# The hand-over between two layers: the first chunk's return trip from memory in two other tiles, and the second chunk's scalings at another place of the last unit

## The chip, the cores and the metric

The kernel runs on one core of one Trainium2 chip. A core has five engines that run side by side, each through its own list of instructions in order: TensorE (PE, with its weight loads shown as PEld), VectorE (DVE), ScalarE (ACT), GpSimd (POOL) and SyncE (SP), which here issues nearly all transfers. The metric is the device time of one execution in microseconds (us); the kernel before has a median of 1962.9 us over 3 runs (1961.62 to 1962.97).

## What is computed

Two layers, each an attention with one shared key and value head and a SwiGLU feed-forward, with a layer norm ahead of each and a residual sum behind it. There are 2048 positions of 448 features, 16 query heads of 28, and a hidden width of 1792.

```python
def _A_ref(x, wq, wk, wv, wo):
    q = (x @ wq).reshape(B, S, H, Dh).transpose(0, 2, 1, 3)
    k = x @ wk
    v = x @ wv
    scores = jnp.einsum("bhqd,bkd->bhqk", q, k) * (Dh ** -0.5)
    p = _softmax(scores, axis=-1)
    o = jnp.einsum("bhqk,bkd->bhqd", p, v)
    return o.transpose(0, 2, 1, 3).reshape(B, S, H * Dh) @ wo

def _B_ref(x, w_gate, w_up, w_down):
    return (_silu(x @ w_gate) * (x @ w_up)) @ w_down

x = A_x
x = x + _A_ref(_layernorm(x), A_wq, A_wk, A_wv, A_wo)
x = x + _B_ref(_layernorm(x), B_w_gate, B_w_up, B_w_down)
x = x + _A_ref(_layernorm(x), A_wq, A_wk, A_wv, A_wo)
x = x + _B_ref(_layernorm(x), B_w_gate, B_w_up, B_w_down)
```

## The kernel before

**Tiling.** The 2048 positions are four chunks `c` of 512, each four tiles of 128 positions. The residual stream stays on chip in `xres`. A product with a weight needs the chunk normalised and turned, features on the partitions, as a high and a low part (`xh`, `xl`) whose sum is the value. A chunk is turned in one of two ways. `flip` turns it on TensorE: the four tiles are scaled into a tile `xn` (line 255 on DVE, with a copy of the last 64 features on POOL, line 257), then for each of four feature slices k four transposes go into one PSUM bank (line 296), and `flipped` takes the high part from the bank on ACT (line 304) and the low part on DVE (lines 309, 312). The other way goes through memory: DVE transposes 32x32 blocks into `xn` (line 260), four transfers write them out to `xt` (line 269), `load` brings them back (line 273), and `cut` makes high and low parts of what came back.

**The feed-forward.** 1792 hidden columns are 14 blocks `fc` in 7 groups of two. In groups 2 to 5 the work is arranged in another way (`blocked`), which uses the four `keys` tiles as operands. Group 6, the last, runs as single units: for each chunk c, for n = 0 and 1, `unit` makes the gate and up products of one block (line 350), then the SiLU on ACT (line 1110), the product with the up half on DVE (line 1111, here called the gating), the high part of the result on ACT (line 1112) and its low part on DVE (line 1115). The down product of a unit is held back in `pend` and issued during the next unit.

**The hand-over.** When the last group of a layer has added a chunk to `xres` and there is a next layer, `hand_over` prepares that chunk for the next attention. Chunk 0 goes through memory: its block transposes come one unit later and its `load` two units later, through a list `soon` whose entries count down at the end of each unit; its `cut` stands in `mid` of the very last unit (group 6, chunk 3, n = 1). Chunk 1 is flipped on TensorE: its four scalings are the function `ready`, and it too has a place in `soon`. The last unit's entry in `soon` that comes first is the one with the first three projections of the next layer.

`unit` runs the list of the place `mid` between the two halves of its gate and up products:

```python
for f in mid[:1]:
    f()
first.pop(0)()
for f in mid[1:]:
    f()
```

and the list `soon` at its end, in the order in which entries were added:

```python
for e in list(self.soon):
    e[0] -= 1
    if e[0] < 0:
        self.soon.remove(e)
        e[1]()
```

**The next layer's projections.** `project` takes pairs (chunk, m) in the order m = 3, 2, 0, 1 of each chunk. Each is 11 matmuls into one bank (line 330). ACT copies the bank to a `stage` tile (line 558), SP sends it to memory as `qd` (line 559) and, for m = 3 and 2, its last rows as `kt` (line 562); for m = 0 and 1 DVE transposes the last rows into `vt` (line 565) and POOL files them in `vsb` (line 568). There are two `stage` tiles, so a third copy waits until the transfers from the first have landed. Ahead of the fourth projection, `turned` flips chunk 1. After that comes the held-back down product of the last unit, and then the projections of chunks 1 to 3.

**What sets the order.** The order on each engine is the order in which the program issues the instructions; nothing reorders them. The banks of a unit and of the projections are taken in turn from a list of four.

**Tiles.** `xn` is a single buffer: each new use of it waits until every reader of the last use is done. `keys` are four tiles of [128, 2, 512], allocated for the whole program. In the next layer the split of `keys[2]` and `keys[3]` comes with its projections 15 and later.

Of the kernel before, what the change touches and what calls it, by code (L numbers as in the profile page):

```python
# [8 lines left out]
F32 = mybir.dt.float32  # L9
# [6 lines left out]
P = 128  # L16
# [36 lines left out]
def forward(  # L53
# [14 lines left out]
    nc = tc.nc  # L68
# [9 lines left out]
    pers = ctx.enter_context(tc.tile_pool(name="pers", bufs=1))  # L78
# [47 lines left out]
    def rows3(dst, src):  # L126
        nc.sync.dma_start(dst[:, 0:3], src[0:384, :].rearrange("(k p) n -> p k n", p=P))
        for rs in (slice(0, 64), slice(64, 128)):
            nc.sync.dma_start(dst[rs, 3], src[384:448, :])
# [18 lines left out]
    keys = [pers.tile([P, 2, 512], F32R, name=f"keys{c}") for c in range(NC)]  # L148
# [77 lines left out]
    def xtile(pool, again=None):  # L226

        return (
            pool.tile([P, 4, 512], F32R, name="xh"),
            pool.tile([P, 3, 512], F32R, name="xl"),  # L230
            again,
        )

    def norm_steps(c, away=None, n=1):


        got = {}

        def stat(t):
            nc.vector.bn_stats(stats[:, 4 * c + t, :], xres[:, 4 * c + t, :])  # L240
            nc.vector.bn_aggr(mv[:, 4 * c + t, :], stats[:, 4 * c + t, :])

        def scale(z):
            m = 4 // n
            rstd = pers.tile([P, 4], F32, name="rstd", bufs=2)[:, 0:m]
            nc.gpsimd.tensor_scalar(rstd, mv[:, 4 * c + m * z : 4 * c + m * z + m, 1], 1.0, EPS, ALU.mult, ALU.add)
            nc.gpsimd.tensor_tensor(rstd, rstd, halfn[:, 0:m], ALU.pow)
            got["r"] = got.get("r", []) + [rstd[:, t : t + 1] for t in range(m)]

        def apply(t):  # L250
            if t == 0:
                got["x"] = pers.tile([P, 4, 512], F32, name="xn")
            got["o"] = (away() if away else got["x"][:, t, :])[:, 0:D]
            i, r = xres[:, 4 * c + t, :], got["r"][t]
            nc.vector.tensor_scalar(got["o"], i, mv[:, 4 * c + t, 0:1], r, ALU.subtract, ALU.mult)
            if not away:
                nc.gpsimd.tensor_copy(got["x"][:, t, D:512], got["o"][:, 384:D])

        def turn(t):
            nc.vector.transpose(side()[:, :, :, t], got["o"].rearrange("p (k s) -> p k s", s=32))  # L260

        def side():
            return got["x"].rearrange("p t n -> p (t n)")[:, 0 : 4 * D].rearrange("p (k s t) -> p k s t", s=32, t=4)

        def send():
            turns.append(dram.tile([D, 512], F32, name=f"xt{len(turns)}"))
            got["xt"] = turns[-1]
            for a in range(4):
                nc.sync.dma_start(
                    got["xt"].rearrange("(k r) n -> r k n", r=32)[:, :, P * a : P * a + P],  # L270
                    side()[32 * a : 32 * a + 32].rearrange("p k s t -> p k (s t)"),
                )

        def load():
            got["raw"] = pers.tile([P, 4, 512], F32, name="xn")
            rows3(got["raw"], got["xt"])

        got["load"] = load
        fs = [lambda t=t: stat(t) for t in range(4)] + [lambda z=z: scale(z) for z in range(n)]
        for t in range(4):  # L280
            fs += [lambda t=t: apply(t)] + [lambda t=t: turn(t)] * bool(away)
        return fs + [send] * bool(away), got
# [3 lines left out]
    def cut(got, tiles, ks=range(4), copy=nc.scalar.copy):  # L286

        for k in ks:
            flipped(tiles, k, got["raw"][:, k, :], copy)

    def flip(got, tiles, ks=range(4)):

# [6 lines left out]
    def flipped(tiles, k, pt, copy, steps=(0, 1)):  # L299

        xh, xl, xd = tiles
        twice = xd if k == 3 else None
        if 0 in steps and twice is None:
            copy(xh[:, k, :], pt)
        elif 0 in steps:
            copy(xh[0:64, k, :], pt[0:64, :])
            copy(xd[64:128, :], pt[64:128, :])
        if 1 in steps and k < 3:
            nc.vector.tensor_tensor(xl[:, k, :], pt, xh[:, k, :], ALU.subtract)
        elif 1 in steps:  # L310
            high = xh[64:128, k, :] if twice is None else xd[64:128, :]
            nc.vector.tensor_tensor(xh[64:128, k, :], pt[64:128, :], high, ALU.subtract)
# [470 lines left out]
    class FeedForward:  # L783
# [251 lines left out]
        def hand_over(self, gi, c):  # L1035

            a = self.nxt
            fs, got = norm_steps(c, None if c else lambda: qraw)
            for f in fs[:5]:
                f()  # L1040
            a.pool = self.stage
            a.X[c] = xtile(xpool if c < 2 else self.xbp)

            def ready():
                for f in fs[5:]:
                    f()
                a.norms[c] = got

            wipe = lambda: nc.gpsimd.memset(qraw, 0.0)
            if c == 0:  # L1050
                self.soon.append([1, lambda: [f() for f in fs[5:9]]])
                self.soon.append([2, lambda: [f() for f in (*fs[9:], got["load"], wipe)]])
                self.mid[gi, 3, 1] = [lambda: None, lambda: cut(got, a.X[c])]
                self.soon.append([5, lambda: [a.project() for _ in range(3)]])
            elif c == 1:
                self.soon.append([3, ready])
            else:
                a.plan[4 * c - 4, 0] = [ready]

# [121 lines left out]
        def rest(self, xb):  # L1181
# [10 lines left out]
            if mixed:  # L1192
                self.lend(mixing)
            cut(self.norms[2], self.X[2])
            third, self.norms[3] = norm_steps(3)
            for f in third[:5]:
# [45 lines left out]
    fs, got = norm_steps(0, n=2)  # L1242
# [28 lines left out]
    for c in range(1, NC):  # L1271
        fs, got = norm_steps(c, n=2)
        n = 4 * c - 4 - (c == 3)
# [40 lines left out]
```

## Time and profile before

| | before |
|---|---|
| median of 3 runs | 1962.9 us (1961.62 to 1962.97) |
| the profiled execution | 1962.7 us |
| its span, first to last instruction | 1960.9 us |
| granted TensorE clock, mean | 1.000 |
| ACT busy | 1339.3 us (68%) |
| DVE busy | 1016.9 us (52%) |
| POOL busy | 771.3 us (39%) |
| transfers | 79.69 MB, mean 41 GB/s |

Times inside the execution are us from the span's start. A row of the timeline reads: start, duration, engine, line of the program, operation, what is written and what is read, shapes, number of instructions merged into the row, and in brackets how long the engine sat idle before it and what released it. A row with several instructions spans from the first one's start to the last one's end. "SPq" rows are issues of transfers; how long the data then take is not in the row. The hand-over from the first layer to the second lies between 960 and 1006 us.

### The profile page before, as it was taken

The page shows a single profiled execution, that of the slowest core. Times are in us where ns is not written, and L with a number is a line of the kernel's source. Part 1 is how long each engine was busy: PE and PEld are TensorE (multiplying, and loading weights), DVE is VectorE, ACT ScalarE, POOL GpSimd, SP SyncE. Part 2 cuts the span into 40 slices and gives each one's busy share as a digit, 9 for nine tenths or more (in the row PEclk, how much of TensorE's full clock was granted, in tenths as well). Part 3 has the DMA queues.
Part 4 walks back from the last instruction along what each step waited for, and adds up shares of the span by engine and source line. Part 5 has one row for each costly group of instructions (what it writes and reads, how often), then busy time and mean ns, then how long its engine had stood idle before and what let it go on. Part 6 is the DMA issues. An engine that isn't in the chain of part 4 may idle for free. (4 is left out here: it accounts for less than half of the span.)

```text
span 1960.9 us, 45644 instructions
## 1 busy us (share of the span) xinstructions
PE 1947.1 (99%) x18307; PEld 1319.9 (67%) x18307; DVE 1016.9 (52%) x1711; ACT 1339.3 (68%) x2353; POOL 771.3 (39%) x997
## 2 busy tenths in 40 slices
PE   9999999999999999999999999999999999999998
PEld 8544545445458999999974444454444688999997
DVE  7434543544435567665654335435444346667653
ACT  4899797998964344444349998979979533444432
POOL 5212111132314868766341221111222167688640
PEclk9999999999999999999999999999999999999999
DMA  5111020121210110011131111102112101110102
GB/s 168 53 30 26 25 49 20 32 59 28 73 33 2 53 33 24 24 33 27 52 112 33 29 31 31 45 12 61 31 50 50 33 6 49 33 32 22 27 17 77
DMA packets 100001, 79.69 MB, mean 41 GB/s; under 512 B 26024, under 2 KB 82984, under 8 KB 99784
## 3 DMA queue, kind: packets, MB, share of 16 engines
q1 hardware_dynamic: 99208, 75.81, 14.3%
q8 instruction: 144, 2.36, 0.5%
q10 hardware_dynamic: 576, 0.92, 0.1%
q14 instruction: 73, 0.60, 0.1%
HBM read 57.15 MB, written 18.74 MB: 39 GB/s over the span
## 5 line engine op out<-in xcount | busy, mean ns | idle before, releaser
L672 PE MATMUL bank<-pt,vsb 128*32 128x512 f32 x4096 | 493.3, 598 | 0.3
L631 PE MATMUL bank<-qstack,keys 32*128 32x512 f32 x1536 | 484.7, 425 | 0.0
L631 PE MATMUL three<-qstack,keys 32*128 32x512 f32 x4608 | 460.6, 425 | 1.5 <-DVE vt L565 1.2
L631 PEld LDWEIGHTS three<-qstack,keys 32*128 32x128 f32 x4608 | 254.4, 182 | 295.0 <-ACT pt L644 179.4
L638 ACT ACTIVATE pt<-three 128x1536 f32<-128x1536 f32 x256 | 372.1, 1454 | 1.2 <-PE bank L672 0.8
L644 ACT ACTIVATE pt<-three 128x1536 f32<-128x1536 f32 x256 | 371.7, 1452 | 0.0
L350 PE MATMUL bank<-xh,wgh 64*128 64x512 f32 x1344 | 364.5, 392 | 0.3 <-DVE sg L1111 0.3
L350 PE MATMUL bank<-wdh,h 64*128 64x448 f32 x1776 | 329.4, 364 | 0.1
L640 DVE COPY raw<-bank 128x512 f32<-128x512 f32 x256 | 177.2, 692 | 226.9 <-PE bank L631 224.6
L350 PE MATMUL bank<-xh,wgl 64*128 64x512 f32 x1020 | 291.8, 390 | 0.0
L682 DVE TENSOR_TENSOR o<-bank,o 128x512 f32<-128x512 f32 x224 | 154.9, 691 | 239.5 <-PE bank L672 234.6
L672 PEld LDWEIGHTS bank<-pt,vsb 128*32 128x32 f32 x4096 | 107.1, 109 | 249.7 <-issue 153.0
L711 POOL TENSOR_TENSOR o<-o 128x512 f32<-128x512 f32 x32 | 41.2, 1287 | 592.6 <-DMA o<-rd 459.3
L357 ACT COPY seen<-bank 128x1 f32<-128x1 f32 x788 | 100.2, 163 | 243.4 <-PE bank L350 182.4
L350 PE MATMUL bank<-xl,wgh 64*128 64x512 f32 x912 | 254.9, 390 | 0.0
L631 PEld LDWEIGHTS bank<-qstack,keys 32*128 32x128 f32 x1536 | 243.4, 183 | 1.2 <-DVE o L682 0.6
L350 PEld LDWEIGHTS bank<-wdh,h 64*128 64x128 f32 x1776 | 237.7, 184 | 9.5 <-issue 2.0
L350 PE MATMUL bank<-wdl,h 64*128 64x448 f32 x888 | 213.2, 366 | 0.0
L350 PEld LDWEIGHTS bank<-xh,wgh 64*128 64x128 f32 x1344 | 200.3, 184 | 11.6 <-DVE sg L1111 0.7
L897 POOL TENSOR_TENSOR xres<-stage,xres 128x448 f32<-128x448 f32 x120 | 151.0, 1269 | 113.0 <-ACT stage L890 112.8
L643 ACT ACTIVATE pt<-bank 128x512 f32<-128x512 f32 x256 | 151.0, 590 | 61.1 <-PE bank L631 60.9
L862 DVE TENSOR_TENSOR xn<-bank,xn 128x512 f32<-128x512 f32 x192 | 126.5, 687 | 125.7 <-PE bank L350 94.7
(202 smaller groups left out, 3085.3 us busy)
## 6 DMA issues: line engine op xcount, KB each, us to landing
o<-rd SPq DMA_DIRECT2D x32, 256.0 KB
qraw<-qd SPq DMA_DIRECT2D x128, 56.0 KB
qd<-stage SPq DMA_DIRECT2D x30, 224.0 KB
xt<-xn SPq DMA_DIRECT2D x28, 224.0 KB
wdr<-in_B_w_down_dram SPq DMA_DIRECT2D x28, 224.0 KB
wr<-in_B_w_gate_dram SPq DMA_DIRECT2D x32, 192.0 KB
wr<-in_B_w_up_dram SPq DMA_DIRECT2D x32, 192.0 KB
xn<-xt SPq DMA_DIRECT2D x7, 768.0 KB
```

The costliest lines, as they stand in the source:

```text
L350: nc.tensor.matmul(po, a, b, start=start, stop=stop, skip_group_check=True)
L357: nc.scalar.copy(seen[:, i : i + 1], po[:, 0:1])
L631: nc.tensor.matmul(three[:, j, :] if j < 3 else one, k[js, kp, ks], q[js, part, :], start=(z == 0), stop=(z == 2), tile_position=(32 * j, 0),)
L638: nc.scalar.activation(pt, three, AF.Exp, scale=SCALE)
L640: nc.vector.tensor_copy(raw, one)
L643: nc.scalar.activation(pt1, one, AF.Exp, scale=SCALE)
L644: nc.scalar.activation(pt, three, AF.Exp, scale=SCALE)
L672: nc.tensor.matmul(po[32 * j : 32 * j + 32, :], vsb[:, n % NT, :], pts[n][j], start=(n == 2 * d), stop=(n > 2 * d), skip_group_check=True,)
L682: nc.vector.tensor_tensor(acc, in_turn(po), acc, ALU.add)
L711: nc.gpsimd.tensor_tensor(rb, oraw, rb, ALU.mult)
L862: plus = lambda out, po, r: tt(by_tile(out), in_turn(po), by_tile(r), ALU.add)
L897: nc.gpsimd.tensor_tensor(r, h[e, t], r, ALU.add)
```

## The change

`load` gets an argument. Without it, it does what it did. With two tiles it issues four transfers in the place of three: feature slices 0 and 1 of `xt` go to the first tile in one transfer, slice 2 to the second tile in one, and the 64 rows of slice 3 twice, to both halves of the partitions, as before. `hand_over` calls it for chunk 0 with `keys[2]` and `keys[3]`, and `cut` reads the slices from there. `ready`, the scalings of chunk 1, leaves `soon` and is appended to the list in `mid` of the last unit, behind the `cut` of chunk 0.

```diff
-        def load():
-            got["raw"] = pers.tile([P, 4, 512], F32, name="xn")
-            rows3(got["raw"], got["xt"])
+        def load(into=None):
+            if into is None:
+                got["raw"] = pers.tile([P, 4, 512], F32, name="xn")
+                rows3(got["raw"], got["xt"])
+                return
+            two, one = (t.bitcast(F32) for t in into)
+            nc.sync.dma_start(two, got["xt"][0:256, :].rearrange("(k p) n -> p k n", p=P))
+            nc.sync.dma_start(one[:, 0], got["xt"][256:384, :])
+            for rs in (slice(0, 64), slice(64, 128)):
+                nc.sync.dma_start(one[rs, 1], got["xt"][384:448, :])
+            got["apart"] = [two[:, 0], two[:, 1], one[:, 0], one[:, 1]]
...
-            flipped(tiles, k, got["raw"][:, k, :], copy)
+            flipped(tiles, k, got["apart"][k] if "apart" in got else got["raw"][:, k, :], copy)
...
-                self.soon.append([2, lambda: [f() for f in (*fs[9:], got["load"], wipe)]])
+                self.soon.append([2, lambda: [f() for f in (*fs[9:], lambda: got["load"](keys[2:4]), wipe)]])
                 self.mid[gi, 3, 1] = [lambda: None, lambda: cut(got, a.X[c])]
                 self.soon.append([5, lambda: [a.project() for _ in range(3)]])
             elif c == 1:
-                self.soon.append([3, ready])
+                self.mid[gi, 3, 1].append(ready)
             else:
                 a.plan[4 * c - 4, 0] = [ready]
```

On DVE, in the last unit of the first layer, the order was as follows. `bank_7095` holds the unit's up product, `bank_7094` the third projection, `h` is the unit's result, `vt` belongs to the third projection, and the rows behind it are chunk 1's.

```order
L309 TENSOR_TENSOR xl<-xn,xh 128x512 x3
L312 TENSOR_TENSOR xh<-xn,xh 64x512
L1111 TENSOR_TENSOR sg<-bank_7095,sg 128x512
L1115 TENSOR_TENSOR h_12398<-sg,h_12398 128x512
L565 STREAM_TRANSPOSE vt<-bank_7094 32x512
L255 TENSOR_SCALAR xn<-xres,mv,rstd 128x448 x4
L309 TENSOR_TENSOR xl<-bank_7095,xh 128x512
L309 TENSOR_TENSOR xl<-bank_7096,xh 128x512
```

With the change, in the same place:

```order
L317 TENSOR_TENSOR xl<-keys_97,xh 128x512 x2
L317 TENSOR_TENSOR xl<-keys_98,xh 128x512
L320 TENSOR_TENSOR xh<-keys_98,xh 64x512
L255 TENSOR_SCALAR xn<-xres,mv,rstd 128x448 x4
L1119 TENSOR_TENSOR sg<-bank_7095,sg 128x512
L1123 TENSOR_TENSOR h_12407<-sg,h_12407 128x512
L573 STREAM_TRANSPOSE vt<-bank_7094 32x512
L317 TENSOR_TENSOR xl<-bank_7095,xh 128x512
L317 TENSOR_TENSOR xl<-bank_7096,xh 128x512
```

The four scalings moved up past the third projection's `vt`, the unit's low part and its gating, to right behind the low parts of chunk 0. Lines below 273 read 8 higher in the changed program, and line 309 became 317.

SP's queue at the return trip, before:

```order
L269 DMA xt_12143<-xn 32x14x128 x4
L127 DMA xn<-xt_12143 128x3x512
L129 DMA xn<-xt_12143 64x512 x2
L559 DMA qd_0_12427<-stage 112x512
L562 DMA kt_0_800<-stage 12x512
L559 DMA qd_0_12427<-stage 112x512
```

and with the change:

```order
L269 DMA xt_12143<-xn 32x14x128 x4
L280 DMA keys_97<-xt_12143 128x2x512
L281 DMA keys_98<-xt_12143 128x512
L283 DMA keys_98<-xt_12143 64x512 x2
L567 DMA qd_0_12436<-stage 112x512
L570 DMA kt_0_800<-stage 12x512
L567 DMA qd_0_12436<-stage 112x512
```

One transfer of three slices became one of two and one of one; nothing behind them moved. TensorE's order is unchanged.

## The prediction

> **What bounds the kernel now.** I read the page's busy shares first, then TensorE's waits over the whole span.
>
> ```profile
> span 1960.9 us, 45644 instructions
> PE 1947.1 (99%) x18307; PEld 1319.9 (67%) x18307; DVE 1016.9 (52%) x1711; ACT 1339.3 (68%) x2353; POOL 771.3 (39%) x997
> ...
> PE bank L296 <- DVE xn L255: 2.1, 1, 2.1
> PE bank L1263 <- POOL ident masks.py:199: 1.9, 1, 1.9
> ```
>
> TensorE is busy for all but 1960.9 - 1947.1 = 13.8 us, and the change leaves its list of instructions alone. So only a gap can be won or made. The longest single wait on record, 2.1 us, is for the very scalings that move: line 296 flips chunk 1, line 255 scales it. The timeline of TensorE shows the place.
>
> ```profile
> 979.21 0.39 PE L330 MATMUL bank<-xh,wh 128*128 128x512 f32 x1
> 984.42 0.39 PE L330 MATMUL bank<-xh,wl 128*128 128x512 f32 x1
> 986.90 2.91 PE L296 MATMUL bank<-ident,xn 128*128 128x128 f32 x16 [2.09 <-DVE xn L255]
> 989.90 0.19 PEld L330 LDWEIGHTS bank<-xh,wh 128*128 128x128 f32 x1 [0.33 <-DVE xl L309]
> 989.90 0.50 PE L330 MATMUL bank<-xh,wh 128*128 128x512 f32 x1
> ```
>
> The third projection ends at 984.42 + 0.39 = 984.81. The 16 transposes begin 2.09 us later and are spread over 2.91 us, and the fourth projection starts at 989.90, held last by a low part (line 309). It takes chunk 0's operands, but its bank is the one that held chunk 1's first slice, so DVE must have read that slice first. From 984.81 to 989.90 are 5.09 us in which TensorE has 16 transposes to do. DVE shows why.
>
> ```profile
> 975.36 1.90 DVE L309 TENSOR_TENSOR xl<-xn,xh 128x512 fp32r<-128x512 f32 x3 [0.58 <-ACT xh L304]
> 977.29 0.69 DVE L312 TENSOR_TENSOR xh<-xn,xh 64x512 fp32r<-64x512 f32 x1
> 978.00 0.69 DVE L1111 TENSOR_TENSOR sg<-bank,sg 128x512 f32<-128x512 f32 x1
> 979.38 0.69 DVE L1115 TENSOR_TENSOR h<-sg,h 128x512 fp32r<-128x512 f32 x1 [0.69 <-ACT h L1112]
> 985.51 0.72 DVE L565 STREAM_TRANSPOSE vt<-bank 32x512 f32<-32x512 f32 x1 [5.44 <-ACT stage L558]
> 986.27 1.85 DVE L255 TENSOR_SCALAR xn<-xres,mv,rstd 128x448 f32<-128x448 f32 x4
> 989.15 1.89 DVE L309 TENSOR_TENSOR xl<-bank,xh 128x512 fp32r<-128x512 f32 x3 [1.04 <-ACT xh L304]
> ```
>
> DVE idles 5.44 us ahead of `vt`, which waits for the third projection, and the scalings are queued behind `vt`: they could have run in that idle time.
>
> **The change part by part.** First the scalings. They move to 977.29 + 0.69 = 977.98, behind the low part of chunk 0. What they read is there by then: the last statistic of chunk 1 leaves POOL at 975.14 + 1.03 = 976.17, and the writers of `xt`, which must have read the old `xn`, have landed before the load is issued at 969.58. The new tiles matter here: in the old `xn` the scalings would have had to wait for the readers of chunk 0 as well.
>
> ```profile
> 975.14 1.03 POOL L247 TENSOR_TENSOR rstd<-rstd,halfn 128x4 f32<-128x4 f32 x1
> 986.37 1.42 POOL L568 COPY vsb<-vt 32x64 f32<-32x64 f32 x4 [10.20 <-DVE vt L565]
> 987.85 0.89 POOL L257 COPY xn<-xn 128x64 f32<-128x64 f32 x4
> 969.58 0.38 SPq L127 DMA_DIRECT2D xn<-xt  x1
> 970.01 1.14 SPq L129 DMA_DIRECT2D xn<-xt  x2
> 980.53 0.32 SPq L559 DMA_DIRECT2D qd<-stage  x1
> 980.90 0.39 SPq L562 DMA_DIRECT2D kt<-stage  x1
> 983.38 0.42 SPq L562 DMA_DIRECT2D kt<-stage  x1
> 985.92 0.71 SPq L419 DMA_DIRECT2D few<-kt  x1
> ```
>
> They end at 977.98 + 1.85 = 979.83, POOL's four copies, now ahead of `vsb` on an engine idle for 10.20 us, about 0.9 us later: 4 us before TensorE asks.
>
> What sets the fourth projection's start then is a chain of rows that all stand here: third projection's end 984.81; its copy on ACT at 984.89; `vt` 0.62 later, 985.51; its end and hand-off 986.27. In the place of the scalings DVE then takes the low part of slice 0. In the trace that step reaches TensorE in 989.90 - 989.15 = 0.75. The start is 986.27 + 0.75 = 987.02 in the place of 989.90: **a gain of 2.88 us**, just the stretch from 986.27 to 989.15 that falls out. Two things must be done by 986.27 and 987.02. ACT's high part of slice 0 comes 0.63 after the first transpose where the flips are fed freely, and takes 989.15 - 988.54 = 0.61 to reach DVE.
>
> ```profile
> 1004.48 1.91 PE L296 MATMUL bank<-ident,xn 128*128 128x128 f32 x16
> 1005.11 2.05 ACT L304 CAST xh<-bank 128x512 fp32r<-128x512 f32 x4 [0.25 <-PE bank L296]
> 1006.14 0.47 PE L330 MATMUL bank<-xh,wh 128*128 128x512 f32 x1
> ```
>
> That is chunk 2, later on. With a first transpose at about 984.87 ACT can begin at 985.50, when the third copy ends too, and DVE may read at 986.11, before 986.27. The 16 transposes end at 984.87 + 1.91 = 986.78, also if the last four wait for `vt` to leave their bank (a quarter of 1.91 after 986.27). So the low part decides. If it did not, the start would be 1006.14 - 1004.48 = 1.66 after the first transpose, 986.53, and the gain 3.37: the upper end.
>
> [...]
>
> Now the cost side. Gating, high and low part of the last unit move back by the 1.85 us on DVE. The low part then ends by 979.38 + 1.85 + 0.69 = 981.92, and the down product needs it only after the fourth projection, so it hides. The flips write the bank that the gating reads: free at 978.00 + 1.85 + 0.69 = 980.54, needed at 984.87. On ACT the high part waits for the gating, and the first stage copy stands behind it.
>
> ```profile
> 974.70 2.19 ACT L304 CAST xh<-xn 128x512 fp32r<-128x512 f32 x4 [0.79 <-DMA xn<-xt]
> 978.73 0.62 ACT L1112 CAST h<-sg 128x512 fp32r<-128x512 f32 x1 [1.35 <-DVE sg L1111]
> 979.92 0.59 ACT L558 COPY stage<-bank 128x512 f32<-128x512 f32 x1 [0.57 <-PE bank L330]
> 984.89 0.59 ACT L558 COPY stage<-bank 128x512 f32<-128x512 f32 x1 [1.89 <-PE bank L330]
> 988.54 2.06 ACT L304 CAST xh<-bank 128x512 fp32r<-128x512 f32 x4 [3.06 <-PE bank L296]
> ```
>
> High part at 980.58 to 981.20, first copy at 981.22 in the place of 979.92: 1.30 late. Its `kt` is issued at 982.20. The third copy reuses that stage tile and waits for the landing. The trace bounds a landing: `few` reads the second `kt`, issued at 983.38, and went out at 985.92, so a `kt` lands within 2.54: 982.20 + 2.54 = 984.74, before 984.89. It hides, by 0.15. If that cover goes, each 0.1 us of a later landing is 0.1 us less gain, since third copy, `vt` and the high parts all queue behind it. The slowest landing nearby is the writing of `xt`:
>
> ```profile
> 963.22 3.05 SPq L269 DMA_DIRECT2D xt<-xn  x4
> SPq L127 <- DMA xt<-xn: 3.1, 1, 3.1
> ```
>
> 3.1 us after the issue, 982.20 + 0.39 + 3.1 = 985.69, costs 0.8 and leaves 2.08: the lower end.
>
> Last the load. Four issues in the place of three, one of some 0.38 more on SP, which then idles to 980.53. ACT's first high part waits 0.79 us for the first, three-slice transfer; a two-slice one can only land sooner, so up to 0.79 is won there, which eases the stage chain above and nothing else. The last pieces can be later by the extra issue, 0.38, while the low part of slice 3, done at 977.98, is used by the tenth matmul of the first projection at 979.21: 1.2 us of cover.
>
> [...]
>
> **Sum.** -2.88, with 2.1 to 3.4 as bounds. Everything behind hangs on TensorE, so it shifts as a block: the chain that ended last runs from the down product straight into the projections of chunk 1.
>
> ```profile
> 995.93 7.77 PE bank L330 x33
> ```
>
> The profiled execution took 1962.7 us, its span and 1.8 around it; 1962.7 - 2.9 = 1959.8. It lies 0.2 below the median of the runs, 1962.9, so I forecast a median of 1960.0.
>
> **The rivals.** (a) *More comes free.* The down product after the fourth projection is slower than the same work elsewhere:
>
> ```profile
> 972.15 0.39 PE L350 MATMUL bank<-wdh,h 64*128 64x448 f32 x2
> 973.38 0.41 PE L350 MATMUL bank<-xh,wgh 64*128 64x512 f32 x2
> 992.62 0.47 PE L350 MATMUL bank<-wdh,h 64*128 64x448 f32 x2
> 995.90 0.50 PE L330 MATMUL bank<-xh,wh 128*128 128x512 f32 x1
> ```
>
> 24 matmuls take 3.28, two times 12 would take 2 x 1.23 = 2.46. If ACT and DVE, freed earlier, close that 0.82 and the full 3.37 is won, the gain is 4.2: 1958.7. Against it: ACT's and DVE's rows there keep their distance to the fourth projection's end. (b) *The stage tile is late*, by the 0.8 above: 1960.8. For it: only 0.15 to spare. (c) *The change doesn't do what it says*: the scalings still wait, for a landing in the last unit or for POOL, until `vt` is done: 1962.9. Against it stand the 976.17 and 969.58 above. (d) *Slower: the four pieces of the load land one after another.* If each took the 3.3 us that `xt` needed from its last issue to the load (963.22 + 3.05 to 969.58), the last would land at 969.58 + 13.2 = 982.8, 8.1 after the 974.70 of now. The 1.2 of cover goes, TensorE starves for 6.9 in the first projection, and less the 2.9 won this is 4.0 slower: 1966.9. It decides against the change from 4.1 us of lateness on. Against it: both halves of slice 3 were issued within 1.14.
>
> **How the numbers follow.** Forecast 0.60, (a) 0.22, (b) 0.07, (c) 0.03, (d) 0.08. About 0.2%, 3.9 us, is what a measurement here can tell from no change. The forecast's 2.9 is short of that by 1.0; medians of runs that spread over 1.3 us carry one fifth of it across, 0.12, and (a) gives 0.20: faster 0.32. The rest of both, less 0.01, with (b) and (c) is 0.59 within the bound; (d) and that 0.01 are 0.09 slower. The range 1958.3 to 1961.8 holds the forecast with its bounds and scatter, (a) and (b), and leaves out (d) and (c).
>
> **What would show it.** Right: the scalings end near 980 on DVE, the transposes follow the third projection within 0.1 us and take about 1.9, the fourth projection starts 2.2 after the third's end, with `xl` still the last releaser, and the wait on line 255 is gone from TensorE's list. Wrong: ACT's third copy starts after 984.9 with a transfer as its releaser (b); the first projection's matmuls show a gap for `xl` or `xh` (d); scalings behind `vt` (c); or the down product under 3 us (a).

## The result and the profile after

| | before | change |
|---|---|---|
| median on the same chip, 19 runs each | 1962.17 us (1960.91 to 1964.43) | 1958.61 us (1957.77 to 1960.33) |
| ratio, 95% interval | | 0.9982 (0.9975 to 0.9989) |
| the profiled execution | 1962.7 us | 1959.8 us |
| its span | 1960.9 us | 1958.0 us |

The median fell by 3.6 us, the profiled execution by 2.9. Forecast were 2.9 for both: 1959.8 for the profiled execution, which is what it took, and a median of 1960.0 (range 1958.3 to 1961.8), which came out 1.4 lower. Half of these 1.4 us is the starting point: the forecast went down from 1962.9, the median of 3 runs, and with 19 runs it is 1962.17, 0.73 lower. So there are two things to explain: why the gap closed as the sum said, and where the other 0.7 us of the medians came from.

First the head of the page of the changed kernel and its list of TensorE's waits (engine, what waited, its releaser; us in total, how often, longest).

```profile
span 1958.0 us, 45644 instructions
PE 1946.5 (99%) x18307; PEld 1312.0 (67%) x18307; DVE 1016.5 (52%) x1711; ACT 1338.3 (68%) x2353; POOL 774.2 (40%) x997
...
PE bank L1271 <- POOL ident masks.py:199: 1.9, 1, 1.9
PE three L639 <- DVE vt L573: 1.2, 2, 0.6
```

TensorE's work is the same, its idle time fell from 13.8 to 1958.0 - 1946.5 = 11.5 us, and the 2.1 us for the scalings are gone from the head of the list. The timeline of TensorE after:

```profile
984.86 0.39 PE L338 MATMUL bank<-xh,wl 128*128 128x512 f32 x1
985.09 1.47 PE L304 MATMUL bank<-ident,xn 128*128 128x128 f32 x12
986.82 0.63 PE L304 MATMUL bank<-ident,xn 128*128 128x128 f32 x4 [0.26 <-DVE vt L573]
987.45 0.19 PEld L338 LDWEIGHTS bank<-xh,wh 128*128 128x128 f32 x1 [0.24 <-DVE xl L317]
987.45 0.50 PE L338 MATMUL bank<-xh,wh 128*128 128x512 f32 x1
990.21 0.47 PE L358 MATMUL bank<-wdh,h 64*128 64x448 f32 x2
993.50 0.51 PE L338 MATMUL bank<-xh,wh 128*128 128x512 f32 x1
...
1031.66 0.50 PE L639 MATMUL three<-qstack,keys 32*128 32x512 f32 x3 [0.60 <-DVE vt L573]
```

The third projection ends at 984.86 + 0.39 = 985.25 and the fourth starts 2.20 later, where it was 5.09. The transposes run on without a wait but for 0.26 us, and what releases the fourth is the low part, as before. From the third projection's end to the first projection of chunk 1 it is now 993.50 - 985.25 = 8.25 us, before 995.90 - 984.81 = 11.09: 2.84 won at this place. The rest of the span adds nothing: it stood 0.44 later at the third projection, and took half a microsecond less in the 965 us behind. The last row is the second group of scores in the next layer, 1031.66 - 985.25 = 46.41 behind the third projection; it serves as a mark further on. DVE and ACT in the same place:

```profile
977.03 0.69 DVE L320 TENSOR_TENSOR xh<-keys,xh 64x512 fp32r<-64x512 f32 x1
977.75 1.78 DVE L255 TENSOR_SCALAR xn<-xres,mv,rstd 128x448 f32<-128x448 f32 x4
979.45 0.68 DVE L1119 TENSOR_TENSOR sg<-bank,sg 128x512 f32<-128x512 f32 x1
985.95 0.72 DVE L573 STREAM_TRANSPOSE vt<-bank 32x512 f32<-32x512 f32 x1 [4.44 <-ACT stage L566]
986.70 1.89 DVE L317 TENSOR_TENSOR xl<-bank,xh 128x512 fp32r<-128x512 f32 x3
```

```profile
974.18 2.20 ACT L312 CAST xh<-keys 128x512 fp32r<-128x512 f32 x4
980.69 0.58 ACT L566 COPY stage<-bank 128x512 f32<-128x512 f32 x1
985.33 0.59 ACT L566 COPY stage<-bank 128x512 f32<-128x512 f32 x1 [1.90 <-PE bank L338]
985.82 2.25 ACT L312 CAST xh<-bank 128x512 fp32r<-128x512 f32 x4
```

The scalings fill a part of DVE's idle time ahead of `vt`, and the low part of chunk 1 now follows `vt` directly. The third stage copy is released by TensorE's bank, 0.08 behind the third projection, and by no transfer.

### The profile page after: what moved, and what is told of

Read it like the earlier page. It is cut to its first block, busy times and chain, and to the rows that moved or that the text cites. A ratio compares the mean times of both kernels' runs of the same rounds, so it can differ in the third digit from the quotient of the medians.

```text
span 1958.0 us, 45644 instructions
## 1 busy us (share of the span) xinstructions
PE 1946.5 (99%) x18307; PEld 1312.0 (67%) x18307; DVE 1016.5 (52%) x1711; ACT 1338.3 (68%) x2353; POOL 774.2 (40%) x997
## 3 DMA queue, kind: packets, MB, share of 16 engines
q8 instruction: 144, 2.36, 0.5%
## 5 line engine op out<-in xcount | busy, mean ns | idle before, releaser
L358 PE MATMUL bank<-xh,wgh 64*128 64x512 f32 x1344 | 355.0, 392 | 0.3 <-DVE sg L1119 0.3
L358 PE MATMUL bank<-wdh,h 64*128 64x448 f32 x1776 | 324.3, 364 | 0.1
L358 PE MATMUL bank<-xh,wgl 64*128 64x512 f32 x1020 | 286.2, 390 | 0.0
L358 PE MATMUL bank<-xl,wgh 64*128 64x512 f32 x912 | 247.9, 390 | 0.0
L358 PEld LDWEIGHTS bank<-wdh,h 64*128 64x128 f32 x1776 | 225.9, 184 | 11.0 <-issue 2.0
L358 PE MATMUL bank<-wdl,h 64*128 64x448 f32 x888 | 204.7, 366 | 0.0
L358 PEld LDWEIGHTS bank<-xh,wgh 64*128 64x128 f32 x1344 | 191.5, 184 | 13.5 <-issue 0.9
```

The source lines that it names most:

```text
L358: nc.tensor.matmul(po, a, b, start=start, stop=stop, skip_group_check=True)
```

## The experiments

Each stands beside runs of the kernel before on the same chip. Lines of the program differ by a few between versions, so the text goes by names.

### The two halves of the change, each alone

The change does two things, new tiles for the load and a new place for the scalings. The first experiment takes the tiles without the place (an edit to the changed kernel), the second the place without the tiles (an edit to the kernel before).

```diff
-                self.mid[gi, 3, 1].append(ready)
+                self.soon.append([3, ready])
```

> The two keys tiles alone: chunk 0 comes back into them by four transfers, but chunk 1's scalings stand behind vt as before. Theory 1 (only the scalings' place ahead of vt counts): no gain, 1962.2 us within the scatter, the fourth projection 5.0 to 5.1 us after the end of the third, TensorE's wait of 2.1 us on the scalings still there. Theory 2 (the tiles carry a share, since they end the sharing of xn and let the first high part start sooner): some of the 2.9 us appears here, time 1959.5 to 1961, and the fourth projection comes 0.5 us or more earlier.

```diff
-                self.soon.append([3, ready])
+                self.mid[gi, 3, 1].append(ready)
```

> The place alone: the scalings stand in the middle of the last unit, chunk 0 comes back into xn by three transfers as before. Theory 1: the readers of chunk 0 are done when DVE gets to the scalings (its own low parts by order, ACT's high parts 1 us earlier), so the single xn costs nothing; fourth projection 2.2 us after the end of the third, time 1959.2 us, as with the whole change within 0.5. Theory 2 (as the prediction says, in the old xn the scalings have to wait for chunk 0's readers): scalings start after 980 us, gating and first stage copy follow, and the gain is under 2 us.

The tiles alone: 1962.91 us (1961.29 to 1963.87), ratio 1.0 (0.9991 to 1.0009). The place alone: 1958.67 us (1957.81 to 1959.81), ratio 0.9977 (0.9968 to 0.9986). The whole gain is the place. DVE's timeline of the kernel with the place alone, where both use the one `xn`, and ACT's row beside it:

```profile
978.08 0.69 DVE L312 TENSOR_TENSOR xh<-xn,xh 64x512 fp32r<-64x512 f32 x1
978.80 1.78 DVE L255 TENSOR_SCALAR xn<-xres,mv,rstd 128x448 f32<-128x448 f32 x4
```

```profile
975.50 2.19 ACT L304 CAST xh<-xn 128x512 fp32r<-128x512 f32 x4 [0.85 <-DMA xn<-xt]
```

The scalings follow the low part of chunk 0 at once, with no wait. The readers of the old `xn` are ACT's casts, done at 975.50 + 2.19 = 977.69, and DVE's own rows just ahead. DVE's own order puts the last readers in front of the next writer here, and its low parts wait for ACT's casts in any case, so the single buffer cost nothing.

The tiles alone left a surprise. TensorE's rows, and the same kernel's windows (stretch, its length, busy time and count of PE, PEld, DVE, ACT, POOL, then the granted TensorE clock, DMA share, GB/s):

```profile
985.05 0.39 PE L338 MATMUL bank<-xh,wl 128*128 128x512 f32 x1
987.53 4.16 PE L304 MATMUL bank<-ident,xn 128*128 128x128 f32 x16 [2.09 <-DVE xn L255]
991.34 0.78 PE L338 MATMUL bank<-xh,wh 128*128 128x512 f32 x1
...
997.82 0.51 PE L338 MATMUL bank<-xh,wh 128*128 128x512 f32 x1
```

```profile
986.00:988.00 2.00, 0.38 (x2) 0.19 (x2) 1.83 (x4) 0.10 (x1) 0.92 (x3) 1.00 0.37 115
988.00:990.00 2.00, 1.81 (x9) 1.43 (x10) 0.96 (x3) 0.59 (x1) 1.27 (x5) 0.75 0.03 2
990.00:992.00 2.00, 2.00 (x10) 1.90 (x10) 1.68 (x3) 1.45 (x3) 0.00 (x0) 0.50 0.00 0
992.00:994.00 2.00, 2.00 (x10) 1.60 (x9) 0.88 (x2) 0.31 (x1) 0.00 (x0) 0.90 0.00 0
```

And the windows of the kernel before in the same columns:

```profile
988.00:990.00 2.00, 1.82 (x15) 1.50 (x14) 0.96 (x3) 1.46 (x4) 0.74 (x4) 1.00 0.00 0
990.00:992.00 2.00, 2.00 (x9) 1.66 (x10) 1.74 (x3) 0.59 (x2) 0.00 (x0) 1.00 0.00 0
```

Both have the same idle time of 2.09 us, but in this execution the granted clock fell to 0.50 behind it. The 16 transposes took 4.16 in the place of 2.91, the fourth projection came 991.34 - 985.44 = 5.90 behind the third, and in all the hand-over lost about 1.3 us (997.82 - 985.44 = 12.38 to chunk 1's first projection, against 11.09). Over the three windows 2 x (0.25 + 0.50 + 0.10) = 1.70 us of the clock are lost, which is 3.4 us at half the clock. The profiled execution of the kernel before had not shown it.

### Another place, and half the work moved

If only the place counts, then any place ahead of `vt` will do, and moving half the scalings should win half. The scalings at the end of the last unit, ahead of the projections' entry and behind gating and low part (on the kernel before):

```diff
-                self.soon.append([3, ready])
+                self.soon.insert(0, [3, ready])
```

> The scalings stay at the end of the last unit, but one place earlier: behind the unit's gating and low part and ahead of the first three projections, so ahead of vt; chunk 0 comes back into xn. Theory 1: DVE is idle there, the scalings end near 982, fourth projection 2.2 us after the end of the third, time as with the whole change (1958.6 to 1959.3); gating and high part are not put back, so ACT's first stage copy comes 0.05 to 0.1 us after the first projection's end as it would without the move, and not 1 us late. Rival (the middle of the unit is needed, since POOL's copies or the flips come too late otherwise): fourth projection 3 us or more after the third's end, gain under 2 us.

Two of the four scalings in `mid`, two behind `vt` (on the changed kernel):

```diff
-                self.mid[gi, 3, 1].append(ready)
+                def late():
+                    for f in fs[7:]:
+                        f()
+                    a.norms[c] = got
+
+                self.mid[gi, 3, 1].append(lambda: [f() for f in fs[5:7]])
+                self.soon.append([3, late])
```

> Two of the four scalings in the middle of the last unit, two behind vt, chunk 0 in the keys tiles. Theory 1 (each scaling behind vt delays the flip of the first slice by its own 0.46 us): fourth projection 4.1 to 4.2 us after the third's end, gain of 0.9 us on the kernel before, 1961.2 us. Rival (what counts is the bank of the last slice or POOL's copies, which wait for vt or the last scaling in any case): all or nothing, 2.2 us or 5.1 us.

The other place: 1959.07 us (1957.76 to 1960.63), ratio 0.998 (0.9971 to 0.9989), the fourth projection again 2.20 behind the third. Half: 1961.59 us (1960.16 to 1963.18), ratio 0.9992 (0.9983 to 1.0001). TensorE's rows of the half:

```profile
985.80 0.39 PE L338 MATMUL bank<-xh,wl 128*128 128x512 f32 x1
...
988.28 2.06 PE L304 MATMUL bank<-ident,xn 128*128 128x128 f32 x14 [1.87 <-DVE xn L255]
990.43 0.50 PE L338 MATMUL bank<-xh,wh 128*128 128x512 f32 x1
```

and DVE's low part:

```profile
989.68 1.89 DVE L317 TENSOR_TENSOR xl<-bank,xh 128x512 fp32r<-128x512 f32 x3 [1.04 <-ACT xh L312]
```

990.43 - 986.19 = 4.24 from the third to the fourth projection: the first two scalings, half of 1.85 us on DVE, are worth 0.85, their own time. The last two are worth 4.24 - 2.20 = 2.04. The rows of the kernel before say why: behind the scalings (986.27 + 1.85 = 988.12) DVE idled another 1.04 us for ACT's high part, which waited for the transposes, which waited for the scalings. With two scalings behind `vt` this wait is still there, 1.04 us as before; with none it falls out. So the 2.88 are 1.85 of work and 1.04 of a wait that the work caused.

### The clock by itself

If the clock gives what the sum lacks, then filling TensorE's idle time with useless work, in the kernel before and with nothing moved, must win that part and leave the gap at 5.1 us. Sixteen transposes of the identity go into the bank that the first flip writes next:

```diff
+            if self.layer and self.seen == 3:
+                own = wide[-1][(turn[wide[-1]] + 1) % len(wide[-1])]
+                for n in range(16):
+                    nc.tensor.transpose(banks[own][:, 0:P], ident, ident)
```

> The kernel before, with 16 transposes of the identity into the first flip's own bank ahead of the flips, whose result is overwritten: TensorE works through 1.75 of the 2.09 us that it idles there. The scalings stay behind vt. Theory 3 (of the measured gain of 3.6 us some 0.7 is not the gap but the clock: in part of the executions the granted clock falls to half behind the gap, as in the profile of the kernel with the tiles alone, where it reads 0.75 and 0.50 from 988 to 992 us): faster than before by 0.4 to 1.0 us in the median, mean granted clock 0.999 or more in each run, and no slice below 1.0 between 980 and 1000 us in the profile; the fourth projection still 5.1 us after the third's end. Rival (the rest of the gain is scatter of the medians): time as before within 0.3 us, clocks of 0.998 in half of the runs.

1961.77 us (1959.98 to 1962.12) against 1962.9 (1961.43 to 1964.03), ratio 0.9992 (0.9983 to 1.0001); the medians differ by 1.13 us, a little more than expected, and the means by 1.27. TensorE's rows:

```profile
985.46 0.39 PE L330 MATMUL bank<-xh,wl 128*128 128x512 f32 x1
985.69 1.91 PE L526 MATMUL bank<-ident 128*128 128x128 f32 x16
987.94 2.91 PE L296 MATMUL bank<-ident,xn 128*128 128x128 f32 x16 [0.34 <-DVE xn L255]
990.93 0.50 PE L330 MATMUL bank<-xh,wh 128*128 128x512 f32 x1
```

The fourth projection starts 990.93 - 985.85 = 5.08 behind the third, as in the kernel before: the work on the path is the same and the idle time is 0.34 in the place of 2.09. The granted clock of the profile is 1.00 from 980 to 1000 us. The interval of the ratio just reaches 1, so this run alone does not settle it; the clock of all runs says more. Each run lists its mean granted clock, to three places. Of the 117 runs of the kernel before in these comparisons 64 show 0.998, with the tiles alone 8 of 11, with half 2 of 11. Of the 129 runs without the long idle time (the 19 of the change above, and eleven each of this one, the place alone, the other place, the change in two repeats, and the five versions below) not one does.

But 0.998 does not count the executions in which the clock falls at the hand-over. In the profiles of the kernel before and of the changed kernel it also reads half at the very end of the span, where TensorE has no work left, for 1.8 us in the one and 2.9 in the other. In the changed kernel:

```profile
1955.00:1957.90 2.90, 0.00 (x0) 0.00 (x0) 0.00 (x0) 0.00 (x0) 0.00 (x0) 0.51 0.05 18
```

This takes 0.0004 and 0.0007 off the mean, and one fall as in the tiles alone takes 1.70 / 1961.5 = 0.0009; neither gives 0.998 alone, 0.0007 and 0.0009 together do. Two other figures say more. Without the long idle time 52 of 129 runs show 1.000, with the kernel before 2 of 117. And the mean of the runs' clocks is 0.9992 to 0.9997 for each version without it, 0.9984 or 0.9985 for each set of the kernel before: lower by about one whole fall per execution. So most executions of the kernel before have the fall, which is worked out from these means; no profile of that kernel caught one. For the same reason the two labels do not price it: with the tiles alone the runs at 0.998 took 1963.12 us on average and the others 1961.55, with half 1962.86 and 1961.11, but in the 117 runs of the kernel before, the largest set, it is 1962.95 and 1962.41.

The change was measured again, to see whether its gain is the 2.9 of the gap or that and the clock's part:

> The change itself once more, on the same chip as the run after it. The traces give 2.9 us for the gap alone; with theory 3 (0.7 to 1.3 us more from executions in which the clock falls behind the gap) the median is 3.4 to 4.2 us below that of the kernel before and the mean granted clock of the runs is 0.0008 to 0.0010 higher. Rival (no clock share): 2.6 to 3.2 us and equal clocks.

1958.18 us (1957.91 to 1959.12) against 1962.52 (1961.18 to 1963.78), ratio 0.9979 (0.997 to 0.9988): 4.3 by the medians, just above the expected range, 4.2 by the means, mean clock 0.9994 against 0.9985.

### The down product ahead of the fourth projection

The last unit's down product takes 3.29 us behind the fourth projection. Its first half could stand between the transposes and the fourth projection, where TensorE waits for the low part:

```diff
-        def project(self):
+        def project(self, wedge=()):
...
+            for f in wedge:
+                f()
...
-                self.nxt.project()
+                self.nxt.project([self.pend.pop(0)])
```

> The whole change, and the first half of the last unit's down product stands between the flips and the fourth projection. It fills the 0.5 us in which TensorE waits for vt and the first low part, and parts the two halves, between which ACT's small copies cost 0.8 us. Theory A: the first projection of chunk 1 begins up to 1.0 us earlier against the end of the third projection than with the change (8.25 us), time 1957.6. Rival: DVE takes vt and the diagonal tile ahead of the additions to xres that free the first projection's bank, and they move behind the fourth projection, which now ends 1.2 us later: the first projection of chunk 1 waits for them, no gain or up to 0.6 us lost, 1958.6 to 1959.2.

1959.86 us (1959.06 to 1962.09), ratio 0.9984 (0.9975 to 0.9993), no better than the change. Chunk 1's first projection came 996.47 - 987.25 = 9.22 behind the third, for its bank was then one that the residual sum of the last unit still had to be read from:

```profile
PE bank L338 <- DVE xres L1019: 1.4, 1, 1.4
```

So the next version sets the turn of the banks, so that this projection gets one that is free:

```diff
             wide.append(ALL)
             if self.layer:
+                turn[ALL] = 3
```

> As the run before it, and the projections of chunk 1 begin on a bank that the flips used and that is long free, so they don't wait for the additions to xres. Theory A and the rival of the run before it both give here: first projection of chunk 1 about 7.2 us after the end of the third projection (8.25 with the change), 1.0 us faster than the change, 1957.6 us. If it isn't, the wait lies elsewhere (ACT's copies between the halves, or a flip of chunk 2 that comes too early for its scalings).

1959.96 us (1959.08 to 1960.31), ratio 0.9984 (0.9975 to 0.9993). Chunk 1's first projection comes 993.02 - 985.32 = 7.70 behind the third, 0.55 earlier than in the change, but a new wait stands further on:

```profile
PE bank L461 <- POOL q L483: 1.1, 1, 1.1
```

POOL's casts of the queries (`q`) come late, behind chunk 3's statistic (lines 246 and 247). The next version puts that statistic off to the place of chunk 3's scalings, and leaves the load in `xn`, since the tiles had been shown to do nothing:

```diff
+            own = 4 if c == NC - 1 else 5
-            for f in fs[:5]:
+            for f in fs[:own]:
                 f()
...
-                for f in fs[5:]:
+                for f in fs[own:]:
                     f()
```

> The scalings in the middle of the last unit with chunk 0 in xn, as in place_only, the first half of the down product between the flips and the fourth projection and the other banks, as in wedge_banks, and POOL's scaling factors of chunk 3 put off to that chunk's own scalings, so that the rounded queries come before them. Theory: the wait of 1.1 us on POOL that ate wedge_banks' gain goes; 0.55 us stay won in the first projection of chunk 1 (7.7 us after the third's end against 8.25), and 0.3 to 0.6 us are left at the first scores: 0.3 to 0.6 us faster than the change. Rival: the scalings of chunk 2 on DVE, queued behind the statistics of chunk 3, now come last (their end at 1000.3 in wedge_banks against flips at 1000.8): same time as the change.

1958.5 us (1957.55 to 1959.74), ratio 0.998 (0.9971 to 0.9989): the wait on the casts is gone, and the time is no better than the change's beside it, 1958.18. The place where it was lost shows at the second group of scores, in TensorE's timeline at 1032.26, 47.27 behind the third projection's end, where the change has 46.41. My reading was that the other banks made the maxima and the last `vt` come last there. So the banks were moved back for the later projections:

```diff
+            if self.layer and self.seen == 9:
+                turn[ALL] = (turn[ALL] + 4) % 8
```

> wedge_full with the turn of the wide banks moved on by four places once nine projections of layer 1 are done, so that from chunk 2's third projection on every product uses the bank that it uses in the change. Theory (the 0.86 us that wedge_full lost at the end of the projections comes from the other banks there: the maxima and the last v^T copies come last on them): the first scores start 45.9 us behind the end of the third projection, where the change has 46.41 (977.x to 1031.66) and wedge_full 47.27, and the median is 0.5 us under the change's, near 1958.0. Rival (the time is lost to VectorE, which has the same work to do in the end wherever the product stands): the first scores start 46.4 us or later behind the third projection, and the median is that of the change.

1959.15 us (1958.65 to 1961.94), ratio 0.9981 (0.9972 to 0.999), and the second group 1032.19 - 985.14 = 47.05 behind the third projection. The reading was wrong. The timeline of its DVE and TensorE shows the real place, ten microseconds earlier:

```profile
1013.75 1.78 DVE L255 TENSOR_SCALAR xn<-xres,mv,rstd 128x448 f32<-128x448 f32 x4 [4.64 <-POOL rstd L247]
```

```profile
1014.32 2.91 PE L304 MATMUL bank<-ident,xn 128*128 128x128 f32 x16
```

The transposes of chunk 3, in the change 1.91 long, are spread over 2.91, since they wait for scalings that wait for the statistic that my own edit had put off: the same stall as the one that the change removes, made anew for another chunk. The remedy is a third place for the statistic, behind the casts: the entry of chunk 1's third projection (the expectation calls it the last). It is put into the version ahead of the last one (`wedge_full` in the expectations), so without the banks' second move.

```diff
-                for f in fs[own:]:
+                for f in fs[5:]:
...
                 a.plan[4 * c - 4, 0] = [ready]
+                if c == NC - 1:
+                    a.plan[6, 0] = [fs[own]]
```

> wedge_full with one thing put elsewhere: POOL's two steps for chunk 3's statistic (line 246 and 247) go to the entry of chunk 1's last projection, ahead of the v copies, and no longer to the entry of chunk 2's first. Theory (the time that wedge_full won at the first projection of chunk 1 was given back because the edit itself put chunk 3's statistic off: in wedge_back's profile DVE's scalings of chunk 3 idled 4.64 us for POOL's line 247, and chunk 3's 16 transposes took 2.91 us where the change has 1.91): the transposes of chunk 3 take 1.91 again, the scores' second group starts 45.9 us behind the third projection's end (the change 46.41, wedge_full 47.27), and the median is 0.5 us under that of the change on the same chip. Rival (VectorE's and POOL's work at the end of the projections sets the first scores wherever the product stands): 46.4 us or more, and the change's median.

And the change beside it on the same chip:

> The change once more, as the measure beside wedge_rstd. By the first theory it is 0.5 us slower than wedge_rstd; by the rival it is the same. Against the kernel before on this chip: 3.5 to 4.3 us faster, as in the runs so far.

The version with the statistic moved: 1958.21 us (1957.39 to 1958.59), ratio 0.9978 (0.9969 to 0.9987); it has no new tiles. The change: 1958.75 us (1957.35 to 1960.11), ratio 0.9982 (0.9973 to 0.9991). TensorE of the former:

```profile
992.87 0.50 PE L338 MATMUL bank<-xh,wh 128*128 128x512 f32 x1
...
1014.12 1.91 PE L304 MATMUL bank<-ident,xn 128*128 128x128 f32 x16
...
1031.01 0.50 PE L642 MATMUL three<-qstack,keys 32*128 32x512 f32 x3 [0.60 <-DVE vt L575]
```

Chunk 3's transposes take 1.91 again, and the second group of scores comes 1031.01 - 985.15 = 45.86 behind the third projection, the expected 45.9; the change in its third profile has 1031.49 - 985.13 = 46.36. So 0.50 us are won in the trace. In the times it is 0.54 by the medians and 0.56 by the means, but the two intervals of the ratio overlap, and the change in its second measurement, on the same chip, took 1958.18 at a ratio of 0.9979: as fast as this version. The trace shows this step up to the second group of scores; that it shortens the whole time is not shown.

## Why the prediction held, and where it did not

- **What bounds the kernel** (TensorE; only a gap can be won): right. The tiles alone, which close no gap, are worth nothing; the place alone is worth all.
- **The size of the gap.** Predicted 2.88, and 2.21 from the third to the fourth projection; measured 2.89 and 2.20. The terms held too: the scalings end at 977.75 + 1.78 = 979.53 (979.83 said), the copy comes 0.08 behind the projection, `vt` 0.62 behind that, and the low part 0.75 ahead of TensorE. The half confirms what it is made of. One sign came out otherwise: the transposes, said to take about 1.9, are spread over 987.45 - 985.09 = 2.36, since the last four wait for `vt` to leave their bank; the low part still comes last.
- **"The new tiles matter here"**: wrong. The step took the single buffer for a wait without asking when its last reader is done. The place alone shows the scalings without a wait in the old `xn`.
- **The first stage copy 1.30 late**: too large. It came at 980.69, where 979.92 + 0.44 = 980.36 would be the old place in this execution: 0.33 late. ACT's first high part no longer waited for the load (974.18, with no idle time noted, where it had been 974.70 after 0.79), so DVE's queue began earlier: its gating stands at 979.45 where 978.00 + 0.44 + 1.85 = 980.29 had been worked out. The prediction had named this as something that eases the stage chain, and did not put it into that sum.
- **Rival (a)**, more comes free: wrong in its mechanism. The down product still takes 3.29, and the transposes are not what decides. That its time, 1958.7, is the one that was measured is luck. **Rival (b)**, the stage tile: refuted by the third copy's releaser. **Rival (c)**: refuted by the missing wait. **Rival (d)**, the four pieces: refuted, since ACT's high parts start 974.18 - 969.94 = 4.24 behind the first issue, where it was 5.12, and the four of them take 2.20 (2.19 before), so no piece was late.

```profile
969.94 0.38 SPq L280 DMA_DIRECT2D keys<-xt  x1
970.41 0.42 SPq L281 DMA_DIRECT2D keys<-xt  x1
970.88 1.10 SPq L283 DMA_DIRECT2D keys<-xt  x2
```

- **The median.** 1960.0 forecast, 1958.61 measured: besides the starting point, the step that failed is a term missing from the sum. The sum was made against one profiled execution, whose mean clock was 1.000, and took for granted that the idle time costs its own length and no more. By the means of the clocks above, the clock falls behind that idle time in most executions of the kernel before. Against the gap's 2.9, the means of the three comparisons of the change are lower by 3.5, 4.2 and 3.7 us, so this term is 0.6 to 1.3 on average; the filled gap without the change gives 1.27 by its means. That the profiled execution, which had no fall, still lay at the median of the runs was luck: behind the second group of scores it took 926.8 us, where the 13 other profiles took 924.1 to 926.3.
- **"About 0.2%, 3.9 us, is what a measurement here can tell from no change"**: too wide. The interval of the 3.6 us, 0.9975 to 0.9989, leaves out 1.

What stays open: only one profile caught the fallen clock at the hand-over, so its cost per execution, 1.3 us, stands on one example, beside the 1.27 of the filled gap, whose interval just reaches 1. What decides in which executions the clock falls was not tried, and no run shows it.

## What to carry to other kernels

When an engine idles ahead of an instruction that waits for another engine, look at what is queued behind that instruction and could have run ahead of it; the price of the wrong order is the queued work's own time, and the wait of everything that hangs on it: here 1.85 us of scalings and 1.04 of a wait behind them. Count a single buffer as a wait only when its last reader ends later than the writer could begin. And after each move ask which statistic, scaling or cast of another chunk has become late: of the versions with the product moved, the second lost its gain to a late cast, the third and fourth to a late statistic of chunk 3.

## What the runs showed of the hardware

The granted clock can fall to 0.50 behind an idle time of TensorE of 2.09 us, and does so in some executions and not in others of kernels with the same gap. In the profile of the tiles alone it read 0.75 in the first 2-us window behind it, 0.50 in the next, 0.90 in the third and 1.00 again from there; in that of the kernel before it read 1.00 in all of them. With an idle time of 1.87 us, in the half, the runs' clocks have a mean of 0.9988, between the kernel before (0.9984 to 0.9985) and the versions without the gap (0.9992 or more); with one of 0.34 us it is 0.9995.
